# Block-recurrent attention with top-1 experts: batches' weights in half-MB parts, one per slot, and deeper buffers for the rounds

## The chip, the cores and the metric

The kernel runs on one core of a Trainium2 chip. The metric is the device time of one execution in microseconds, as the median of several runs. Engines are called PE (matrix), DVE (vector), ACT (scalar), POOL (GpSimd) and SP (which here only issues transfers).

## The reference

There are eight batches with eight heads each. Every head has 512 tokens `x` and 32 states, 64 wide. Tokens attend to the states and states attend to the tokens. The results are joined to 544 rows of 512 per batch (512 token rows, 32 state rows), 4352 rows in all. Every row then goes to one of eight experts, by the largest gate logit, and through that expert's two layers.

```python
scores = x @ state.T / 8;   xread = softmax(scores) @ state      # 512 token rows
scores2 = state @ x.T / 8;  sread = softmax(scores2) @ x         # 32 state rows
x = concat([xread, sread]) as (4352, 512)
e = argmax(x @ w_gate);     gate = softmax(x @ w_gate)[e]
out = gate * (relu(x @ w1[e]) @ w2[e])                           # w1: 8 x 512 x 1024, w2: 8 x 1024 x 512
```

All numbers are 32-bit floats. One expert's `w1` has 2 MB, and so has its `w2`.

## The kernel before, in words

**Token rows by batch.** The kernel takes the expert that most token rows of a batch chose (`eb`) for the whole batch; a branch at the end would mend batches in which rows chose otherwise, and with this data it isn't entered. It never forms `xread`: `states_w1` multiplies the states with `w1` (tile `G`, 32 matmuls named pG), `up` multiplies the attention weights `aT` with `G` (ph, 32 matmuls of 512 columns) and applies relu into `hT`, and `down` multiplies `hT` with `w2` (py, four column blocks `c` of 16 matmuls in two halves), after which ACT scales a block into `y` and issues its store. One batch is `down(b)`, with `states_w1(b + 1)` in it, and then `up(b + 1)`. `w1` has one buffer, `w2` two, `y` three.

**Slots.** `others()` is one generator that holds all the rest of the work in program order. `down` advances it eight times (after the first half and after the end of each block) and `up` four times, so a batch has 12 slots. Slots 0 to 27 are the attention of batches 1 to 7 (`first`, `front`, `back`). Slots 28 and 29 sort the state rows by expert and scatter them to DRAM (`sort_states`), and then `change_pools` gives the attention's memory to the rounds.

**State rows by rounds.** Three rounds of 128 sorted state rows follow, four groups of 32 rows with an expert each. A round reads 8 tiles of `w1` (tag s1) and 8 of `w2` (tag s2). Each tile is 1 MB and comes by four transfers of 256 KB (`s<-in_moe_w_dram`), one per group. `rounds` first fetches as many tiles as there are buffers (`S1B, S2B = 3, 3`) with the gathered rows `xg` between them, lets five slots go by, and then has `round_x` (ptx), four `round_up` (pgh, 16 matmuls) with a slot between two of them, relu, `round_h` (pth), and four times two `round_down` (pgy, 8 matmuls each). After each `round_up` two s1 tiles are fetched, after each `round_down` one s2 tile.

**Order.** Engines keep the program's order (`InOrder`). All reads are issued on SP, the `y` stores on ACT. Before, `load_w1` and `load_w2` issue 2 MB at once, in `between(c)` after block 2 (block 3 of batch 0) and after `down`. `between(c)` runs after the slot at the end of a block:

```python
store(c, py)
if insert:
    next(insert, None)      # the slot's work
if between:
    between(c)              # states @ w1 of the next batch, load of w1 after it
```

Four PSUM banks, `bank(...)`, serve py, ph, pG and the attention's small results in turn; `states_w1` takes all four, and each is free again when ACT has copied it to `G`.

**Start.** `begin()` chooses batch 0's expert from the states alone, loads its `w1` in two column halves, then `x` and states of batch 1, then `w2`, and writes blank rows to DRAM (four transfers), all on SP.

In the profile every instruction stands under line 48, the helper that records it, so groups are told by their tiles.

Of the kernel before, what the change touches and what calls it, by code (L numbers as in the profile page):

```python
# [9 lines left out]
FP32 = mybir.dt.float32  # L10
# [10 lines left out]
def kernel(  # L21
# [36 lines left out]
    DM = H * D  # L58
# [12 lines left out]
    NG = 16  # L71
    NR = NG // 4
    NRS = 3
    S1B, S2B = 3, 3
    FAR = 1 << 20

    PSUM = bass.MemoryType.PSUM
# [2 lines left out]
    wpool = ctx.enter_context(tc.tile_pool(name="wpool", bufs=1))  # L80

    ss_dram = dram.tile([NG * 32, XW], I32)


    ffn = tc.alloc_tile_pool(name="ffn", bufs=1)
# [22 lines left out]
    load_x(0, sp)  # L108
    wg = const.tile([128, NDC, E], FP32)
    act.dma_start(out=wg[:], in_=moe_w_gate.rearrange("(c p) e -> p c e", p=128))  # L110
    warm = const.tile([128, 1], FP32)
    dve.memset(warm[:], 0.0)
    act.activation(warm[:], warm[:], AF.Exp)
# [40 lines left out]

    aT = const.tile([128, B, 4, 2, 128], FP32)

    stT = const.tile([128, B, H, 2, NS], FP32)
    NX = B * NC  # L160
    lgs = const.tile([128, NST, E], FP32)
    oh = const.tile([128, NX + NST, E], BF16)
# [35 lines left out]

    def turn_states(b, copy):

        to = stT[:, b].rearrange("p h u n -> p (h u n)")
        dve.transpose(to[0:64], st2[b][:].rearrange("p h d -> p (h d)"))
        copy(to[64:128], to[0:64])

    def states_gates(b):

        pg = [bank("pg") for _ in range(2)]
        for q in range(4):
            for g in range(2):
                pe.matmul(pg[g][ts(q, 32), 0:E], lhsT=stT[ts(g, 64), b, 2 * q + g, 0, :],  # L210
                          rhs=wg[ts(g, 64), q, :], start=True, stop=True, skip_group_check=True)
        for g in range(2):
            act.copy(gst[:, b, g, 0:E], pg[g][:, 0:E])

    def scores(b, xt):

        pc = ps_c.tile([128, 4, 512], FP32, tag="c", name="pc")
        for g in range(2):
            for u in range(2):
                for q in range(4):  # L220
                    for i in range(4):
                        pe.matmul(pc[ts(q, 32), i, ts(g, 128)], lhsT=stT[ts(i, 32), b, 2 * q + g, u ^ (i % 2), :],
                                  rhs=xt[ts(i, 32), 2 * q + g, :, u, :],
                                  start=(u == 0), stop=(u == 1), skip_group_check=True)
        return pc
# [95 lines left out]
            load_states(b + 2, sp, sp)  # L321

    def turn_read(b, i=ALL):
        dve.transpose(aT[:, b, i].rearrange("p i g s -> p (i g s)"),
                      soft[b][0][:, i].rearrange("p i b n -> p (i b n)"))

    def logits_x(b):
        pl = bank("pl")[:, 0:128]
        for g in range(2):
            for i in range(4):  # L330
                pe.matmul(pl[ts(i, 32)], lhsT=gst[:, b, g, :], rhs=aT[:, b, i, g, :],
                          start=(g == 0), stop=(g == 1), skip_group_check=True)
# [79 lines left out]
    def begin():  # L412

        nonlocal G, hT
        turn_states(0, act.copy)
        states_gates(0)
        pr = bank("prg")[:, 0:E]
        for g in range(2):
            pe.matmul(pr, lhsT=ones_f[:], rhs=gst[:, 0, g, 0:E], start=(g == 0), stop=(g == 1), skip_group_check=True)
        xt, sx = new_xt(), new_sx()  # L420
        turn_x(0, xt, slice(0, 4))
        most(0, pr)
        e = expert_of(eb, 0)
        load_w1(0, e, 2)
        load_x(1, sp)
        load_states(1, sp, sp)
        load_w2(0, e)
        for r in range(NR):
            sp.dma_start(out=ss_dram[ts(r, 128)], in_=blank[:])
        turn_x(0, xt, slice(4, 8))  # L430
        pc = scores(0, xt)
        one, two = slice(0, 2), slice(2, 4)
        soft[0] = (sx,)
        turn_scores(pc, sx, 0)
        turn_scores(pc, sx, 1)
        less_max(sx, one, dve)
        exponential(sx, one)
        turn_scores(pc, sx, 2)
        turn_scores(pc, sx, 3)
        over_sum(sx, one, dve)  # L440
        turn_read(0, one)
        G = states_w1(w1s[0], stT[:, 0])
        less_max(sx, two, dve)
        exponential(sx, two)
        nm = write_max(pc)
        over_sum(sx, two, dve)
        turn_read(0, two)
        hT = new_hT()
        up(G, aT[:, 0], hT, one)
        soft[0] += write_weights(pc, nm)  # L450
        xt, sx = new_xt(), new_sx()
        turn_x(1, xt, slice(0, 4))
        turn_x(1, xt, slice(4, 8))
        turn_states(1, act.copy)
        exps, gates = logits_x(0)

        def beside():
            states_gates(1)
            pc = scores(1, xt)
            for i in range(4):  # L460
                turn_scores(pc, sx, i)
# [12 lines left out]
            yield  # L474
        up(G, aT[:, 0], hT, two, beside(), 4)

    def expert_of(table, i, engines=(SP,)):
        _, (e,) = nc.values_load_multi_w_load_instructions(
# [3 lines left out]

    w1s, w2s = {}, {}

    def load_w1(b, e, parts=1):
        w1s[b] = wpool.tile([128, NDC, F], FP32, tag="w1", name="w1t")
        for k in range(parts):
            f = ts(k, F // parts)
            sp.dma_start(out=w1s[b][:, :, f], in_=moe_w1[ds(e, 1)].rearrange("o (c p) f -> p (o c) f", p=128)[:, :, f])

    def load_w2(b, e):
        w2s[b] = wpool.tile([128, NFC, DM], FP32, tag="w2", bufs=2, name="w2t")
        sp.dma_start(out=w2s[b][:], in_=moe_w2[ds(e, 1)].rearrange("o (c p) f -> p (o c) f", p=128))

    def run(*gens):

# [17 lines left out]
    def states_w1(w1t, st):  # L514

        G = ffn.tile([128, 2, F], FP32, tag="G", name="G")
        for k in range(2):
            pg = [bank("pG") for _ in range(2)]
            for q in range(4):
                for g in range(2):  # L520
                    pe.matmul(pg[g][ts(q, 32), :], lhsT=st[ts(g, 64), 2 * q + g, 0, :],
                              rhs=w1t[ts(g, 64), q, ts(k, 512)], start=True, stop=True, skip_group_check=True)
            for g in range(2):
                act.copy(G[:, g, ts(k, 512)], pg[g][:])
        return G
# [17 lines left out]
    def down(hT, w2t, store, insert=None, between=None):  # L543
        for c in range(NC):
# [5 lines left out]
                    next(insert, None)  # L550
            store(c, py)
            if insert:
                next(insert, None)
            if between:
                between(c)

    def store_batch(b):
        rows = out[ds(b * SO, S)].rearrange("(p c) f -> p c f", c=NC)
# [172 lines left out]
    def rounds(r0, r1):  # L731
# [3 lines left out]
        fetch(S1B, 0)  # L735
        round_in(r0)
        fetch(0, S2B)
        for _ in range(5):
            yield
        for r in range(r0, r1):  # L740
            round_x(r)
# [14 lines left out]
            for f in range(0, NFC, 2):  # L756
                for i in range(2):
                    round_down(r, f + i)
                    fetch(0, 1)
                yield  # L760
                if r + 1 < r1:
                    yield
            round_out(r)


# [2 lines left out]
    def first():  # L768
# [6 lines left out]
        write_rows(1)  # L775
        choose(1)
        e1 = expert_of(eb, 1)
        load_w1(1, e1)
        load_w2(1, e1)
        gates()  # L780
        yield
        for b in range(2):
            turned[b] = turn_rows(b)

    turned = {}

    def others():

# [9 lines left out]
    def batch(b):  # L798
# [3 lines left out]
        def between(c):  # L802
            nonlocal G
            if c == (1 if b else 2) and b + 1 < B:
                G = states_w1(w1s[b + 1], stT[:, b + 1])
            if c == (2 if b else 3) and b + 2 < B:
                load_w1(b + 2, expert_of(eb, b + 2))

        down(hT, w2s[b], store_batch(b), work, between)
        if b + 2 < B:  # L810
            load_w2(b + 2, expert_of(eb, b + 2))
        if b + 1 < B:
            hT = up(G, aT[:, b + 1], new_hT(), insert=work)

    work = others()
    for b in range(B):
        batch(b)
# [8 lines left out]
    with tc.If(number(rest_i, B * S + NG) > 0):  # L826
# [3 lines left out]
        with tc.If(number(left_i, B * S) > 0):  # L830
# [18 lines left out]
            with tc.For_i(0, n_pairs, 1):  # L849
# [15 lines left out]
                bb = expert_of(pb, 0, [DVE])  # L865
                load_w1("x", e)
                load_w2("x", e)
                a_x = late["sst"].tile([128, 1, 4, 2, 128], FP32, tag="s1", bufs=S1B, name="a_x")
                dve.tensor_copy(out=a_x[:], in_=aT[:, ds(bb, 1)])
                st_x = late["sst"].tile([128, 1, H, 2, NS], FP32, tag="s2", bufs=S2B, name="st_x")  # L870
                dve.tensor_copy(out=st_x[:], in_=stT[:, ds(bb, 1)])
# [16 lines left out]
                def store(c, py):  # L888
# [5 lines left out]
                down(up(states_w1(w1s["x"], st_x[:, 0]), a_x[:, 0], new_hT()), w2s["x"], store)  # L894
            fix.release()

    for pool in (late["ps_t"], late["ps_g"], late["sst"], ps_p, ffn):
# [31 lines left out]
```

## Time and profile before

| | |
|---|---|
| median of 3 runs | 503.45 us (501.69 to 507.53) |
| profiled execution | 502.99 us, its span 501.2 us |
| PE busy | 465.6 us, 93% of the span |
| DVE, ACT, POOL busy | 119.2, 123.9, 33.9 us |
| moved by DMA | 105.77 MB, 211 GB/s over the span |

PE is the engine that is nearly always busy; the rest is idle time before its instructions, which the timeline gives in brackets with what ended it. A group of matmuls that waits inside for its operands shows as a longer group, not as idle time. The 1.8 us between span and time lie outside the profile.

### The profile page before, as it was taken

How to read it: one execution, taken by the hardware profiler on the slowest of the kernel's cores; microseconds unless marked ns; L12 is line 12 of the kernel's file. 1: busy time of each engine (PE TensorE's matmuls, PEld its weight loads, DVE VectorE, ACT ScalarE, POOL GpSimd, SP SyncE). 2: the span in 40 equal slices, each digit the busy share in tenths (PEclk: the TensorE clock that was granted, in tenths of full speed). 3: DMA queues.
4: the chain of work that ended last, by engine and by line, in shares of the span. 5: the costliest groups of instructions: out<-in, count | busy, mean ns of one | idle time of the engine just before them, and what ended most of it. 6: DMA issues, size and time to landing. Idle time of an engine off the chain costs nothing.

```text
span 501.2 us, 8606 instructions
## 1 busy us (share of the span) xinstructions
PE 465.6 (93%) x3445; PEld 208.1 (42%) x3445; DVE 119.2 (24%) x302; ACT 123.9 (25%) x257; POOL 33.9 (7%) x39
## 2 busy tenths in 40 slices
PE   2699899999899999984999999998999999999995
PEld 2386555455355544431334333432433343343342
DVE  4747565656547623100000000000000000000000
ACT  1244143541415422220032112022120221311101
POOL 1000032230202210100000000000000000000000
PEclk9999999999999999998799999999999999999999
DMA  4942397943535001899769968599558998319211
GB/s 106 355 152 73 95 320 226 337 112 122 190 122 193 4 27 43 279 366 384 272 212 329 391 221 284 180 382 364 196 190 293 397 307 264 118 34 343 72 42 45
DMA packets 63821, 105.77 MB, mean 211 GB/s; under 512 B 11935, under 2 KB 21151, under 8 KB 63776
## 3 DMA queue, kind: packets, MB, share of 16 engines
q1 hardware_dynamic: 57696, 95.64, 56.0%
q10 hardware_dynamic: 5680, 8.47, 4.7%
q0 software_dynamic: 400, 1.05, 0.6%
q8 instruction: 29, 0.48, 0.4%
q14 instruction: 16, 0.13, 0.1%
HBM read 94.13 MB, written 10.75 MB: 209 GB/s over the span
## 4 chain that ended last, share of the span: by engine, by line
PE 73%; DMA 15%; DVE 4%; SPq 3%; issue 2%; ACT 1%; POOL 0%; ACTq 0%; DVEq 0%; POOLq 0%
PE py L48 39%; PE ph L48 15%; DMA s<-in_moe_w_dram 9%; PE pgy L48 5%; DMA w1t<-in_moe_w_dram 4%; PE pgh L48 4%; PE pG L48 3%; PE pc L48 3%; SPq L48 3%; PE pw L48 2%; PE pt L48 2%; DVE xt L48 1%; DMA xg<-ss_dram 1%; DMA st<-in_state_dram 1%; PE pl L48 1%
## 5 line engine op out<-in xcount | busy, mean ns | idle before, releaser
L48 PE MATMUL py<-w2t,hT 128*128 128x512 f32 x512 | 230.8, 601 | 2.5 <-ACT G L48 2.0
L48 PEld LDWEIGHTS py<-w2t,hT 128*128 128x128 f32 x512 | 94.4, 191 | 126.6 <-issue 112.2
L48 PE MATMUL ph<-aT,G 128*128 128x512 f32 (+1 forms) x288 | 117.6, 559 | 0.0
L48 PEld LDWEIGHTS ph<-aT,G 128*128 128x128 f32 x288 | 54.1, 194 | 55.6 <-issue 52.8
L48 ACT ACTIVATE y<-py,gw 128x512 f32<-128x512 f32 x32 | 22.0, 687 | 211.1 <-PE py L48 197.2
L48 ACT ACTIVATE hT<-ph 128x512 f32<-128x512 f32 (+1 forms) x72 | 39.2, 550 | 93.7 <-PE ph L48 93.6
L48 DVE COPY shT<-pth 128x512 f32<-128x512 f32 x3 | 2.1, 692 | 160.6 <-PE pth L48 160.6
L48 PE MATMUL pgh<-s,sxT 128*32 128x512 f32 x192 | 30.0, 619 | 9.4 <-DMA s<-in_moe_w_dram 9.4
L48 PE MATMUL pgy<-s,shT 128*32 128x512 f32 x192 | 27.5, 599 | 0.6 <-DMA s<-in_moe_w_dram 0.6
L48 DVE TENSOR_SCALAR ys<-pgy,xg 128x512 f32<-128x512 f32 x3 | 2.3, 752 | 91.9 <-PE pgy L48 91.9
L48 PE MATMUL pG<-w1t,stT 64*32 64x512 f32 x256 | 18.4, 653 | 4.2 <-DMA w1t<-in_moe_w_dram 4.2
L48 POOL DMA_INDIRECT out_dram<-ys,xg x3 | 2.9, 971 | 263.2 <-DVE ys L48 102.9
L48 DVE STREAM_TRANSPOSE xt<-x_nat 128x1024 f32<-128x1024 f32 x16 | 19.5, 1227 | 1.1 <-DMA x_nat<-in_x_dram 1.1
L48 PE MATMUL pc<-xt,stT 32*32 32x128 f32 x1024 | 17.0, 295 | 2.8 <-issue 1.4
L48 ACT COPY G<-pG 128x512 f32<-128x512 f32 x32 | 16.5, 599 | 11.4 <-PE pG L48 11.4
L48 PEld LDWEIGHTS pgh<-s,sxT 128*32 128x32 f32 x192 | 6.2, 110 | 30.6 <-DMA s<-in_moe_w_dram 17.3
L48 DVE STREAM_TRANSPOSE sx<-pc 128x256 f32<-128x256 f32 x32 | 11.7, 419 | 26.4 <-PE pc L48 26.4
L48 PEld LDWEIGHTS pc<-xt,stT 32*32 32x32 f32 x1024 | 13.5, 107 | 4.1 <-DVE xt L48 1.8
L48 PEld LDWEIGHTS pgy<-s,shT 128*32 128x32 f32 x192 | 6.1, 109 | 20.2 <-issue 14.7
L48 POOL TENSOR_TENSOR sx<-sx,mx 128x1024 f32<-128x1024 f32 x6 | 11.5, 1910 | 34.8 <-DVE mx L48 34.8
L48 DVE STREAM_TRANSPOSE aT<-sx 128x1024 f32<-128x1024 f32 (+1 forms) x9 | 10.1, 1127 | 12.4 <-POOL sx L48 12.3
L48 POOL TENSOR_TENSOR sx<-sx,sm 128x1024 f32<-128x1024 f32 x6 | 11.5, 1912 | 23.0 <-DVE sm L48 19.4
(118 smaller groups left out, 214.0 us busy)
## 6 DMA issues: line engine op xcount, KB each, us to landing
s<-in_moe_w_dram SPq DMA_DIRECT2D x192, 256.0 KB, 5.2
w2t<-in_moe_w_dram SPq DMA_DIRECT2D x8, 2048.0 KB, 12.9
w1t<-in_moe_w_dram SPq DMA_DIRECT2D x7, 2048.0 KB, 10.3
x_nat<-in_x_dram SPq DMA_DIRECT2D x16, 512.0 KB, 5.6
out_dram<-y ACTq DMA_DIRECT2D x32, 256.0 KB, 3.4
w1t<-in_moe_w_dram SPq DMA_DIRECT2D x2, 1024.0 KB, 6.8
ss_dram<-blank SPq DMA_DIRECT2D x4, 257.0 KB, 8.5
xg<-ss_dram SPq DMA_DIRECT2D x3, 257.0 KB, 4.6
```

Of the source, the lines that this page charges most:

```text
L48: ins = getattr(self.engine, name)(*args, **kw)
```

## The change

Batches' weights: `w1_parts` and `w2_parts` give four transfers of half a MB each (`w1` by rows of 128, so a row of 4 KB stays whole; `w2` by two rows of 2 KB). They stand in a list, `lazy`, and each slot issues one of them after its other work. `w1(b + 2)` is put there after block 1 (block 3 of batch 0), `w2(b + 2)` after `down`. Batch 0's `w1` keeps its two halves; `w1` of batch 1 is issued at once. `states_w1` runs ahead of the slot's work at the end of a block. The rounds have 5 and 4 buffers, wait 7 slots, and the last round has the slots of the others. The space comes from the attention: `aT` of batches 0 to 2 and all transposed states `stT` lie in its pool; a packed copy of the states, `stG`, is made by two POOL copies per batch for `states_w1`; and since the branch at the end needs `aT` of any batch, each is also written to DRAM (`at_dram`, 512 KB per batch, on SP). In `begin`, states of batch 1 are loaded at the very start, `w2` comes right behind `w1`, and `x` of batch 1 is issued on ACT behind the first exponential.

```diff
-    S1B, S2B = 3, 3
+    S1B, S2B = 5, 4
+    at_dram = dram.tile([B, 128, 1024], FP32)
@@ start
     act.dma_start(out=wg[:], in_=moe_w_gate.rearrange("(c p) e -> p c e", p=128))
+    load_states(1, sp, sp)
@@ turn_states
+        stT[b] = att.tile([128, H, 2, NS], FP32, tag="stT", bufs=2, name="stT")
         dve.transpose(to[0:64], st2[b][:].rearrange("p h d -> p (h d)"))
         copy(to[64:128], to[0:64])
+        for g in range(2):
+            gp.tensor_copy(out=stG[ts(g, 64), b], in_=stT[b][:].rearrange("p (q g) u n -> p g u q n", g=2)[ts(g, 64), g, 0])
@@ turn_read
+        if b not in aT:
+            aT[b] = att.tile([128, 4, 2, 128], FP32, tag="aT", bufs=NE, name="aTe")[:]
...
+        if i.stop == 4:
+            sp.dma_start(out=at_dram[b], in_=aT[b].rearrange("p i g s -> p (i g s)"))
@@ begin
-        load_w1(0, e, 2)
-        load_x(1, sp)
-        load_states(1, sp, sp)
-        load_w2(0, e)
+        at_once(w1_parts(0, e, 2))
+        at_once(w2_parts(0, e))
...
         exponential(sx, one)
+        load_x(1, act)
...
-        G = states_w1(w1s[0], stT[:, 0])
+        G = states_w1(w1s[0], stG[:, 0])
@@
+    def w1_parts(b, e, cols=1):
+        t = w1s[b] = wpool.tile([128, NDC, F], FP32, tag="w1", name="w1t")
+        rows = moe_w1[ds(e, 1)].rearrange("o (c p) f -> p (o c) f", p=128)
+        f = F // cols
+        return [lambda k=k: sp.dma_start(out=t[:, :, ts(k, f)], in_=rows[:, :, ts(k, f)]) for k in range(cols)] if cols > 1 else \
+            [lambda k=k: sp.dma_start(out=t[:, k], in_=rows[:, k]) for k in range(NDC)]
+    def w2_parts(b, e):
+        t = w2s[b] = wpool.tile([128, NFC, DM], FP32, tag="w2", bufs=2, name="w2t")
+        rows = moe_w2[ds(e, 1)].rearrange("o (c p) f -> p (o c) f", p=128)
+        return [lambda k=k: sp.dma_start(out=t[:, ts(k, 2)], in_=rows[:, ts(k, 2)]) for k in range(NFC // 2)]
@@ down
             if insert:
+                step = between(c)
+                next(step)
                 next(insert, None)
-            if between:
-                between(c)
+                next(step)
@@ rounds
-        for _ in range(5):
+        for _ in range(7):
             yield
...
-                if r + 1 < r1:
-                    yield
+                yield
@@ first
-        load_w1(1, e1)
-        load_w2(1, e1)
+        at_once(w1_parts(1, e1))
+        lazy.extend(w2_parts(1, e1))
@@ batch
             if c == (1 if b else 2) and b + 1 < B:
-                G = states_w1(w1s[b + 1], stT[:, b + 1])
-            if c == (2 if b else 3) and b + 2 < B:
-                load_w1(b + 2, expert_of(eb, b + 2))
+                G = states_w1(w1s[b + 1], stG[:, b + 1])
+            yield
+            if c == (1 if b else 3) and b + 2 < B:
+                lazy.extend(w1_parts(b + 2, expert_of(eb, b + 2)))
+            yield
-        down(hT, w2s[b], store_batch(b), work, between)
+        down(hT, w2s[b], store_batch(b), slots, between)
         if b + 2 < B:
-            load_w2(b + 2, expert_of(eb, b + 2))
+            lazy.extend(w2_parts(b + 2, expert_of(eb, b + 2)))
...
+    def with_weights():
+        while True:
+            next(work, None)
+            if lazy:
+                lazy.pop(0)()
+            yield
```

## Rows read from the trace of the kernel before

**Rows 1.** The page: busy time of the engines, and the chain that ended last.

```profile
PE 465.6 (93%) x3445; PEld 208.1 (42%) x3445; DVE 119.2 (24%) x302; ACT 123.9 (25%) x257; POOL 33.9 (7%) x39
PE 73%; DMA 15%; DVE 4%; SPq 3%; issue 2%; ACT 1%; POOL 0%; ACTq 0%; DVEq 0%; POOLq 0%
```

**Rows 2.** Timeline of PE, rounds: start, us, operation, count, [idle before <- releaser].

```profile
216.94 0.63 PE L48 MATMUL ptx<-ident,xg 128*128 128x128 f32 x4 [1.89 <-DMA s<-in_moe_w_dram]
...
220.93 1.92 PE L48 MATMUL pgh<-s,sxT 128*32 128x512 f32 x16
222.78 7.13 PE L48 MATMUL py<-w2t,hT 128*128 128x512 f32 x16
...
238.26 3.90 PE L48 MATMUL pgh<-s,sxT 128*32 128x512 f32 x8 [7.34 <-DMA s<-in_moe_w_dram]
242.08 7.77 PE L48 MATMUL py<-w2t,hT 128*128 128x512 f32 x16
...
284.34 3.08 PE L48 MATMUL pgy<-s,shT 128*32 128x512 f32 x8 [0.55 <-DMA s<-in_moe_w_dram]
...
349.37 3.45 PE L48 MATMUL pgh<-s,sxT 128*32 128x512 f32 x8 [2.05 <-DMA s<-in_moe_w_dram]
...
453.57 3.02 PE L48 MATMUL pgy<-s,shT 128*32 128x512 f32 x16
```

**Rows 3.** Windows: stretch, us, busy by engine, granted clock, DMA share, GB/s.

```profile
200.84:225.47 24.63, 22.74 (x69) 9.48 (x68) 1.75 (x12) 6.05 (x10) 2.14 (x2) 1.00 0.94 327
...
197.70:204.70 7.00, 7.00 (x21) 3.18 (x18) 4.36 (x28) 0.90 (x2) 2.14 (x2) 1.00 0.42 132
...
222.80:238.30 15.50, 8.16 (x29) 3.15 (x26) 0.00 (x0) 0.69 (x1) 0.00 (x0) 0.83 1.04 381
...
212.70:222.20 9.50, 7.61 (x30) 3.01 (x32) 0.00 (x0) 2.97 (x5) 0.00 (x0) 1.00 1.01 366
```

**Rows 4.** Timeline of SP's issues before the longest wait, and ACT's store among them.

```profile
220.34 0.39 SPq L48 DMA_DIRECT2D w1t<-in_moe_w_dram  x1
221.30 0.38 SPq L48 DMA_DIRECT2D w2t<-in_moe_w_dram  x1
222.82 3.73 SPq L48 DMA_DIRECT2D xg<-ss_dram  x1
226.82 4.25 SPq L48 DMA_DIRECT2D s<-in_moe_w_dram  x5
...
237.42 6.74 SPq L48 DMA_DIRECT2D s<-in_moe_w_dram  x11
...
230.67 0.36 ACTq L48 DMA_DIRECT2D out_dram<-y  x1
```

**Rows 5.** Timelines of PE and ACT around states @ w1 of batches 1 and 2.

```profile
72.95 1.10 PE L48 MATMUL pw<-x_nat,a2T 128*32 128x64 f32 x64
...
74.42 1.95 PE L48 MATMUL pG<-w1t,stT 64*32 64x512 f32 x32
...
126.90 2.36 PE L48 MATMUL pG<-w1t,stT 64*32 64x512 f32 x32
131.25 3.70 PE L48 MATMUL py<-w2t,hT 128*128 128x512 f32 x8 [1.99 <-ACT G L48]
...
130.62 2.04 ACT L48 COPY G<-pG 128x512 f32<-128x512 f32 x4
```

**Rows 6.** Timelines of PE and ACT, start: first products with w1.

```profile
19.70 1.96 PE L48 MATMUL pG<-w1t,stT 64*32 64x512 f32 x16 [2.35 <-DMA w1t<-in_moe_w_dram]
21.59 8.81 PE L48 MATMUL ph<-aT,G 128*128 128x256 f32 x32
...
17.44 1.07 ACT L48 COPY G<-pG 128x512 f32<-128x512 f32 x2 [0.94 <-PE pG L48]
```

**Rows 7.** Timeline of POOL: one of eight copies of states.

```profile
54.67 0.60 POOL L48 COPY stT<-stT 64x512 f32<-64x512 f32 x1 [51.75 <-DVE stT L48]
```

**Rows 8.** All transfers of the rounds' weights: time from issue to landing.

```profile
DMA to landing us min/median/max: 2.4/5.2/12.6
```

More of the change, by code (lines that the diff above doesn't have):

```diff
@@ L153 @@
         dve.tensor_scalar(tok_s[:, g:g + 1], tmp_p[:], float(4 * g * SO + S), None, ALU.add)
-    aT = const.tile([128, B, 4, 2, 128], FP32)
-    stT = const.tile([128, B, H, 2, NS], FP32)
+    NE = 3
+    aTl = const.tile([128, B - NE, 4, 2, 128], FP32)
+    aT = {b: aTl[:, b - NE] for b in range(NE, B)}
+    stT = {}
+    stG = const.tile([128, B, 4, NS], FP32)
     NX = B * NC
@@ L199, in turn_states @@
     def turn_states(b, copy):
[L201 removed]
+        stT[b] = att.tile([128, H, 2, NS], FP32, tag="stT", bufs=2, name="stT")
+        to = stT[b][:].rearrange("p h u n -> p (h u n)")
         dve.transpose(to[0:64], st2[b][:].rearrange("p h d -> p (h d)"))
         copy(to[64:128], to[0:64])
+        for g in range(2):
+            gp.tensor_copy(out=stG[ts(g, 64), b], in_=stT[b][:].rearrange("p (q g) u n -> p g u q n", g=2)[ts(g, 64), g, 0])
     def states_gates(b):
@@ L209, in states_gates @@
             for g in range(2):
-                pe.matmul(pg[g][ts(q, 32), 0:E], lhsT=stT[ts(g, 64), b, 2 * q + g, 0, :],
+                pe.matmul(pg[g][ts(q, 32), 0:E], lhsT=stT[b][ts(g, 64), 2 * q + g, 0, :],
                           rhs=wg[ts(g, 64), q, :], start=True, stop=True, skip_group_check=True)
@@ L221, in scores @@
                     for i in range(4):
-                        pe.matmul(pc[ts(q, 32), i, ts(g, 128)], lhsT=stT[ts(i, 32), b, 2 * q + g, u ^ (i % 2), :],
+                        pe.matmul(pc[ts(q, 32), i, ts(g, 128)], lhsT=stT[b][ts(i, 32), 2 * q + g, u ^ (i % 2), :],
                                   rhs=xt[ts(i, 32), 2 * q + g, :, u, :],
@@ L323, in turn_read @@
     def turn_read(b, i=ALL):
-        dve.transpose(aT[:, b, i].rearrange("p i g s -> p (i g s)"),
+        if b not in aT:
+            aT[b] = att.tile([128, 4, 2, 128], FP32, tag="aT", bufs=NE, name="aTe")[:]
+        dve.transpose(aT[b][:, i].rearrange("p i g s -> p (i g s)"),
                       soft[b][0][:, i].rearrange("p i b n -> p (i b n)"))
+        if i.stop == 4:
+            sp.dma_start(out=at_dram[b], in_=aT[b].rearrange("p i g s -> p (i g s)"))
     def logits_x(b):
@@ L330, in logits_x @@
             for i in range(4):
-                pe.matmul(pl[ts(i, 32)], lhsT=gst[:, b, g, :], rhs=aT[:, b, i, g, :],
+                pe.matmul(pl[ts(i, 32)], lhsT=gst[:, b, g, :], rhs=aT[b][:, i, g, :],
                           start=(g == 0), stop=(g == 1), skip_group_check=True)
@@ L448, in begin @@
         hT = new_hT()
-        up(G, aT[:, 0], hT, one)
+        up(G, aT[0], hT, one)
         soft[0] += write_weights(pc, nm)
@@ L474, in beside @@
             yield
-        up(G, aT[:, 0], hT, two, beside(), 4)
+        up(G, aT[0], hT, two, beside(), 4)
     def expert_of(table, i, engines=(SP,)):
@@ L483, with at_once @@
     w1s, w2s = {}, {}
[L485 to L493, printed above, removed]
+    def w1_parts(b, e, cols=1):
[8 more added lines that the diff above has]
+        return [lambda k=k: sp.dma_start(out=t[:, ts(k, 2)], in_=rows[:, ts(k, 2)]) for k in range(NFC // 2)]
+    def at_once(parts):
+        for p in parts:
+            p()
     def run(*gens):
@@ L520, in states_w1 @@
                 for g in range(2):
-                    pe.matmul(pg[g][ts(q, 32), :], lhsT=st[ts(g, 64), 2 * q + g, 0, :],
+                    pe.matmul(pg[g][ts(q, 32), :], lhsT=st[ts(g, 64), q, :],
                               rhs=w1t[ts(g, 64), q, ts(k, 512)], start=True, stop=True, skip_group_check=True)
@@ L783, in first @@
             turned[b] = turn_rows(b)
-    turned = {}
+    turned, lazy = {}, []
     def others():
@@ L804, in between @@
             if c == (1 if b else 2) and b + 1 < B:
-                G = states_w1(w1s[b + 1], stT[:, b + 1])
-            if c == (2 if b else 3) and b + 2 < B:
-                load_w1(b + 2, expert_of(eb, b + 2))
-        down(hT, w2s[b], store_batch(b), work, between)
+                G = states_w1(w1s[b + 1], stG[:, b + 1])
[4 more added lines that the diff above has]
+        down(hT, w2s[b], store_batch(b), slots, between)
         if b + 2 < B:
-            load_w2(b + 2, expert_of(eb, b + 2))
+            lazy.extend(w2_parts(b + 2, expert_of(eb, b + 2)))
         if b + 1 < B:
-            hT = up(G, aT[:, b + 1], new_hT(), insert=work)
+            hT = up(G, aT[b + 1], new_hT(), insert=slots)
+    def with_weights():
[4 more added lines that the diff above has]
+            yield
+    slots = with_weights()
     work = others()
@@ L864 @@
                 e = expert_of(px, 0)
[L865 to L871, printed above, removed]
+                bb = expert_of(pb, 0, [SP, DVE])
+                at_once(w1_parts("x", e))
+                at_once(w2_parts("x", e))
+                a_x = late["sst"].tile([128, 4, 2, 128], FP32, tag="s1", bufs=S1B, name="a_x")
+                sp.dma_start(out=a_x[:].rearrange("p i g s -> p (i g s)"),
+                             in_=at_dram[ds(bb, 1)].rearrange("o p s -> p (o s)"))
+                st_x = late["sst"].tile([128, 1, 4, NS], FP32, tag="s2", bufs=S2B, name="st_x")
+                dve.tensor_copy(out=st_x[:], in_=stG[:, ds(bb, 1)])
                 g_x = fix.tile([128, NC, 1], FP32)
@@ L893, in store @@
                         in_=y[:], in_offset=None, bounds_check=NTOK - 1, oob_is_err=False)
-                down(up(states_w1(w1s["x"], st_x[:, 0]), a_x[:, 0], new_hT()), w2s["x"], store)
+                down(up(states_w1(w1s["x"], st_x[:, 0]), a_x[:], new_hT()), w2s["x"], store)
             fix.release()
```

## The prediction

> **What bounds the kernel now.** I read the page first: PE is busy for 465.6 us of the 501.2 us span, and the chain that ended last is PE for 73% and transfers for 15% [rows 1]. Beside PE and its weight loads no engine is busy for a third of the span. So the time is PE's work, plus what PE waits. The change removes no matmul; it can only take away waits or add some. So I read PE's timeline for groups with idle time before them, and for groups that are longer than others of their kind, and noted which wait ended each.
>
> Three places stand out. First, the rounds. A round_up without waits is a group of 16 in 1.92 us, so 8 take 0.96 us; a block of py takes 7.13 us [rows 2]. Against these:
> - the first round_x waits 1.89 us (for xg: the releaser named is a tile of weights, but the matmul reads xg);
> - the second round_up waits 7.34 us, its second half then takes 3.90 instead of 0.96, and the py block behind it 7.77 instead of 7.13: 7.34 + 2.94 + 0.64 = 10.92 us;
> - a round_down half waits 0.55 us and takes 3.08: 2.67 us;
> - a round_up half waits 2.05 us and takes 3.45: 4.54 us;
> - four groups have no idle time but are longer; the one shown takes 3.02 instead of 1.92, 1.10 us, and with the other three (1.31, 0.49 and 0.60) it is 3.50 us.
> The sum is 1.89 + 10.92 + 2.67 + 4.54 + 3.50 = 23.5 us. The longest wait has its cause in SP's timeline: `w1` and `w2` of batch 4, 4 MB, are issued at 220.34 and 221.30, ahead of the s1 tile that PE waits for, which is issued from 226.82 [rows 4]. In that stretch the transfers run at 381 GB/s [rows 3], so 4.2 MB are 11 us in front of the tile. And the granted clock's mean over that stretch is 0.83, after PE had begun to wait.
>
> Second, pG of batch 2, in batch 1's `down`: its group takes 2.36 instead of 1.95 us, and py waits 1.99 us behind it, because ACT copies `G` only from 130.62 on, behind the attention's exponentials of that slot [rows 5]. That is 2.40 us. Third, the start, where PE waits for the halves of batch 0's `w1` [rows 6]; the change doesn't shorten that.
>
> **The rounds, part by part.** *More buffers.* With three s1 buffers, after a round_up one tile of the next is there and the other has to be issued, moved and landed within two slots. With five, both are there and the fetch has until the round_up after that: two slots and a round_up more, about 9 us, or 3.4 MB at 381 GB/s. With four s2 buffers instead of three the same holds for a pair of round_down. *Parts.* 2 MB at 381 GB/s are 5.5 us ahead of a tile; half a MB is 1.4 us. *Is there bandwidth?* From 200.84 on the rounds read 48 tiles (50 MB), batches 4 to 7 some 17 MB, and stores take 5 MB: 72 MB, or 190 us at 381 GB/s of the 270 us that are left. So the waits come from order and depth, not from bytes, and I take all 23.5 us as removed, except at the start of the rounds.
>
> *The start of the rounds.* Now 5 + 4 tiles (9.4 MB) are issued in one slot on SP, and three of the four parts of `w1` of batch 4 come behind them in SP's order. What must land by the last of these: 9.4 MB of tiles, 0.3 of xg, 0.5 of scatter, 0.5 of stores, 1.6 of parts: 12.3 MB. Before, the first 24.63 us moved 327 GB/s, 8.05 MB [rows 3]; the other 4.3 MB at 381 GB/s take 11.2 us, which is 236.7, and about 237.7 with the landing. PE comes to this `states_w1` when? Round_x would have run at 216.94 - 1.89 = 215.05 [rows 2]; from there half a 7.13 remains of `up`, then two blocks of `down`, ptx and a round_up: 3.6 + 14.2 + 0.5 + 1.92, so 235.3. The wait is 237.7 - 235.3 = 2.4; I take +2.5 us. Its bounds are 0 (at 381 GB/s throughout it lands at 234) and some 10 us, the first rival. `w2` of batch 4 (5.5 us more) lands near 243 and the next s1 pair near 249, and PE needs the second tile of it at 250.3: just in time.
>
> *Seven slots, and four more slots in the last round.* Two more slots are 7 us at least, which covers the 1.89 us for xg. The rounds end in slot 88 of 92 instead of 83, with three halves of py (10.7 us) behind the last round_down; its DVE scaling and store wait for no slot, so the tail doesn't grow. PE's work is the same in another order: 0.
>
> **The rest.** *States @ w1 first.* Its four copies come on ACT ahead of the slot's exponentials, and the slot's other matmuls give them time. This removes the 2.40 us: -2.4, with 0.4 more if batch 3's pG, as long in the trace, shortens too. Price: batch 1's own `w1` is wanted earlier by pw and pl, 74.42 - 72.95 = 1.47 us, and before it had no idle time [rows 5]; between 0 and 1.47, I take 0.5.
>
> *Batch 1's x on ACT.* Here the change adds a wait. The rows show how many transfers are in flight: behind w2t at 221.30 come xg, five of s and one store on ACT, and then SP issues nothing until 237.42 [rows 4], though the next tile has no part in w2t. So a transfer waits for the eighth before it, on whichever engine. In `begin` the order after w1 is four parts of w2, four blanks, the two halves of x: x's halves wait for w2's first and second part, and ACT stands still with the copies of `G` and the next exponential queued behind. w1's second half is there at 19.70 [rows 6]; 1.4 us per part gives 21.1 and 22.5, and with the issue 23.0. The copies that ran at 17.44 (1.07 us) would then end at 24.1, and ph start there instead of at 21.59: +2.5 us. If x's issue comes ahead of the blanks in that order, the wait is for something long landed: 0. I take 1.5, nearer to the written order.
>
> *Transposed states, packed copies, aT to DRAM.* Two POOL copies per batch of a quarter of the columns of one that takes 0.60 us [rows 7]; nothing waits for POOL just behind them: 0 to 0.6 us each if they were on the path, taken at 0, as `states_w1` comes half a batch later. Eight writes of 0.5 MB are 1.4 us of transfer each, in the attention's stretch. SP waits there for DVE's transpose, with the slot's part and the next state-row writes behind it; these wait for the same stretch of work anyway. At most 1.4 us on a tie, twice; I take 0.3 in all. The states of batch 1 at the start: behind batch 0's x, 0.
>
> **Sum**, against the profiled execution of 502.99 us (the median of the runs, 503.45, is 0.1% above it): 502.99 - 23.5 + 2.5 - 2.4 + 0.5 + 1.5 + 0.3 = 481.9. I predict 482 us.
>
> **A rule against it.** Where the rounds' 256 KB transfers run alone, from 212.70 to 222.20, they move 366 GB/s; the stretch with the two 2 MB ones in it moves 381 [rows 3]. The Trainium skill ("DMA: Bandwidth & Descriptors", "Rules for kernel authors") asks for 128 partitions and at least 1 MiB per transfer for the highest bandwidth; these parts have half of that. By that rule it is the fourth rival; the two rows leave 4% for it, since transfers of a quarter of that size queue behind each other without a gap.
>
> **Rivals.**
> 1. *The start of the rounds still starves.* The 12.3 MB move at 280 GB/s instead of 341: 44 us, 245.8 with the landing, a wait of 10.5 us, and the clock falls as it did before (0.83, 0.64 us on the next block and more on the half round), with the next s1 pair 2 us late. 482 + 8 + 3 = 493. For it: 132 GB/s from 197.70 to 204.70, against it: 327 over the whole start [rows 3]. 14%.
> 2. *The waits move and don't vanish*, because transfers are what bounds the rounds. Then deeper buffers only shift them: 499 to 503 us. For it: a DMA share of 1.04 where PE waited [rows 3]; against it the 72 MB in 270 us above. 7%.
> 3. *Slower: the burst blocks batch 4's w1.* One place, as in 1, but the burst keeps the poor rate of its first microseconds, since scatter, store and tiles meet there. It decides the sign below 216 GB/s: 12.3 MB then take 57 us and PE waits over 21 us more. At 200 GB/s it is 61.5 us, a wait of 28 us and half clock behind it: 508. 4%.
> 4. *Half-MB parts don't overlap.* The shortest landing of a 256 KB transfer is 2.4 us [rows 8], so a part alone takes some 3.1 us instead of 1.4. That binds where parts lie behind the burst: three of w1, 5 us, and four of w2, 7 us, of which 3 are slack: 482 + 9 = 491. 5%.
>
> **How the numbers follow.** The forecast has 70%, between 476 (no new wait at all) and 488 (the start at +2.5, the rounds' start at +5, ties in the attention). A change under 1%, 5 us, could not be told from none in this kernel. Faster by over 1%: the forecast, rivals 1 and 4, 0.89; within 1%: rival 2, 0.07; slower: rival 3, 0.04. The range from 475 to 494 holds the forecast and most of rivals 1 and 4.
>
> **What would show it.** In the changed profile, PE should have no idle time over 1 us before pgh or pgy, and their groups of 16 should take 1.92; the clock should stay at 1.00 through 225 to 250. There should be one wait of 1 to 5 us before pG of batch 4, ended by w1t. Batch 1's py should not wait for `G`. On ACT, x's issue in the start should stand for some 5 us ahead of the copies of `G`, with ph from 22 to 24. The prediction is wrong if a wait over 5 us is left in the rounds, or if PE's busy time itself grows.

## The result

The changed kernel takes 483.67 us (median of 4 runs, 482.35 to 485.41), the kernel before beside it 504.38 us (4 runs, 501.69 to 507.53): a ratio of 0.9589, interval 0.9523 to 0.9655. In a second comparison, with other runs of both, it was 480.73 against 501.73 us, 0.9557, 0.949 to 0.9625. The forecast was 482, with 475 to 494 as its range. The profiled execution took 485.41 us, its span is 483.6 us, and the granted clock is 1.00 over all of it.

### The profile page after: what moved, and what is told of

Same layout as the page of the kernel before. It is cut to its first block, busy times and chain, and to the rows that moved or that the text cites. A ratio compares the mean times of both kernels' runs of the same rounds, so it can differ in the third digit from the quotient of the medians.

```text
span 483.6 us, 8760 instructions
## 1 busy us (share of the span) xinstructions
PE 457.8 (95%) x3445; PEld 206.1 (43%) x3445; DVE 119.4 (25%) x302; ACT 123.5 (26%) x257; POOL 38.6 (8%) x55
## 4 chain that ended last, share of the span: by engine, by line
PE 80%; DMA 11%; DVE 4%; issue 2%; ACT 1%; SPq 1%; POOL 1%; ACTq 0%; POOLq 0%; DVEq 0%
PE py L48 40%; PE ph L48 20%; DMA s<-in_moe_w_dram 5%; PE pgy L48 5%; PE pgh L48 4%; DMA w1t<-in_moe_w_dram 3%; PE pc L48 3%; PE pG L48 2%; PE pt L48 2%; PE pw L48 2%; DMA wg<-in_moe_w_gate_dram 1%; DVE xt L48 1%; DMA out_dram<-y 1%; SPq L48 1%; PE pl L48 1%
## 5 line engine op out<-in xcount | busy, mean ns | idle before, releaser
L48 PE MATMUL ph<-aTl,G 128*128 128x512 f32 x160 | 71.5, 597 | 0.0
L48 PEld LDWEIGHTS ph<-aTl,G 128*128 128x128 f32 x160 | 29.6, 190 | 40.2 <-issue 39.7
L48 PE MATMUL ph<-aTe,G 128*128 128x256 f32 (+1 forms) x128 | 46.3, 514 | 0.0
L48 PEld LDWEIGHTS ph<-aTe,G 128*128 128x128 f32 x128 | 24.9, 202 | 16.6 <-issue 13.7
L48 PE MATMUL pG<-w1t,stG 64*32 64x512 f32 x256 | 21.6, 654 | 4.6 <-DMA w1t<-in_moe_w_dram 4.4
L48 PE MATMUL pgh<-s,sxT 128*32 128x512 f32 x192 | 23.1, 598 | 0.0
L48 PE MATMUL pgy<-s,shT 128*32 128x512 f32 x192 | 23.1, 598 | 0.0
L48 PEld LDWEIGHTS pG<-w1t,stG 64*32 64x32 f32 x256 | 4.6, 109 | 18.9 <-issue 12.9
```

Source lines behind the costliest of these rows:

```text
L48: ins = getattr(self.engine, name)(*args, **kw)
```

## The profile after

The page of the changed kernel: busy time by engine; the chain that ended last; three groups (busy, mean ns | idle before them).

```profile
PE 457.8 (95%) x3445; PEld 206.1 (43%) x3445; DVE 119.4 (25%) x302; ACT 123.5 (26%) x257; POOL 38.6 (8%) x55
...
PE 80%; DMA 11%; DVE 4%; issue 2%; ACT 1%; SPq 1%; POOL 1%; ACTq 0%; POOLq 0%; DVEq 0%
...
L48 PE MATMUL pG<-w1t,stG 64*32 64x512 f32 x256 | 21.6, 654 | 4.6 <-DMA w1t<-in_moe_w_dram 4.4
...
L48 PE MATMUL pgh<-s,sxT 128*32 128x512 f32 x192 | 23.1, 598 | 0.0
L48 PE MATMUL pgy<-s,shT 128*32 128x512 f32 x192 | 23.1, 598 | 0.0
```

PE has the same 3445 matmuls, but is busy for 7.8 us less, and its idle time fell from 35.6 to 25.8 us [rows 1]. Both come from waits: a group that waits inside for its operands counts as busy, and so does one that runs slower behind a wait (from 234 to 242 us of the kernel before, the granted clock was 0.50, the lower level of 1.2 GHz). The rounds' two kinds of group have no idle time left, and 12 groups of 16 at 1.92 us make the 23.1 us of each. What is new is in pG: it is busy for 21.6 us where it was 18.4. Of the 4.6 us idle before it 0.46 are new, at batch 4; the rest is the start's, which the kernel before had too (4.2).

PE's timeline at the start of the rounds, answering [rows 2]: start, us, operation, count, [idle before].

```profile
226.08 0.63 PE L48 MATMUL ptx<-ident,xg 128*128 128x128 f32 x4 [1.65 <-DMA s<-in_moe_w_dram]
...
230.07 1.92 PE L48 MATMUL pgh<-s,sxT 128*32 128x512 f32 x16
231.93 7.13 PE L48 MATMUL py<-w2t,hT 128*128 128x512 f32 x16
238.99 1.37 PE L48 MATMUL pG<-w1t,stG 64*32 64x512 f32 x8
240.59 1.05 PE L48 MATMUL pG<-w1t,stG 64*32 64x512 f32 x4 [0.22 <-DMA w1t<-in_moe_w_dram]
241.88 1.91 PE L48 MATMUL pG<-w1t,stG 64*32 64x512 f32 x20 [0.24 <-DMA w1t<-in_moe_w_dram]
243.71 1.92 PE L48 MATMUL pgh<-s,sxT 128*32 128x512 f32 x16
```

The second round_up, which waited 7.34 us before, now takes 1.92 with nothing ahead of it. Two waits are left: 1.65 us before the first round_x, and `states_w1` of batch 4, which comes in pieces as the parts of its `w1` land. It lasts from 238.99 to 243.79, 4.80 instead of 1.95 us, so 2.85.

SP's issues in that stretch, answering [rows 4], and the window of [rows 3] again.

```profile
203.29 15.40 SPq L48 DMA_DIRECT2D s<-in_moe_w_dram  x20
219.01 0.33 SPq L48 DMA_DIRECT2D xg<-ss_dram  x1
219.60 12.69 SPq L48 DMA_DIRECT2D s<-in_moe_w_dram  x16
232.63 1.86 SPq L48 DMA_DIRECT2D w1t<-in_moe_w_dram  x3
236.46 2.26 SPq L48 DMA_DIRECT2D w2t<-in_moe_w_dram  x4
```

```profile
222.80:238.30 15.50, 13.85 (x47) 5.58 (x46) 0.00 (x0) 1.27 (x2) 0.00 (x0) 1.00 1.03 379
```

The transfers are as busy as before (379 GB/s), yet PE is busy for 13.85 of the 15.50 us instead of 8.16, at a granted clock of 1.00 (2.4 GHz) instead of a mean of 0.83. What SP's rows show is the price: xg is issued only when 20 transfers of s1 are, and the three parts of `w1` only when 36 of both kinds are.

PE's timeline around states @ w1 of batches 1 and 2, answering [rows 5], and after it SP's issues of batch 1's weights (first the changed kernel, then the one before).

```profile
74.30 3.63 PE L48 MATMUL pG<-w1t,stG 64*32 64x512 f32 x32
...
130.16 0.70 PE L48 MATMUL py<-w2t,hT 128*128 128x512 f32 x1 [1.35 <-issue]
130.78 1.95 PE L48 MATMUL pG<-w1t,stG 64*32 64x512 f32 x32
...
133.60 3.70 PE L48 MATMUL py<-w2t,hT 128*128 128x512 f32 x8
```

```profile
66.49 2.65 SPq L48 DMA_DIRECT2D w1t<-in_moe_w_dram  x4
```

```profile
64.74 0.40 SPq L48 DMA_DIRECT2D w1t<-in_moe_w_dram  x1
```

Batch 2's pG is 1.95 us and py waits no longer for `G`. Batch 1's pG takes 3.63, 1.68 us more: PE comes to it before pw and pl, while its `w1` now takes four issues, which last 2.65 us instead of 0.40. The whole `w1` landed 9.0 us after its issue, at 73.8, 0.7 us ahead of pG; the last of the four parts lands 7.2 us after its own, at 76.0, when pG has been running for 1.7 us.

The start, PE and ACT, answering [rows 6].

```profile
8.04 0.33 PE L48 MATMUL pg<-wg,stT 64*32 64x8 f32 x16 [8.04 <-DMA wg<-in_moe_w_gate_dram]
...
20.43 1.96 PE L48 MATMUL pG<-w1t,stG 64*32 64x512 f32 x16 [1.85 <-DMA w1t<-in_moe_w_dram]
22.32 9.26 PE L48 MATMUL ph<-aTe,G 128*128 128x256 f32 x32
```

```profile
16.69 0.95 ACTq L48 DMA_DIRECT2D x_nat<-in_x_dram  x2
18.64 1.07 ACT L48 COPY G<-pG 128x512 f32<-128x512 f32 x2 [1.33 <-PE pG L48]
```

The two issues of x take 0.95 us on ACT, and the copy behind them waited for PE's pG, not for them. Still ph starts 0.73 us later than before: the first instruction of PE waited until 8.04, for the gate's weights, where it began at 7.23 before, with DVE's `xt` as the last that it waited for.

## Experiments

The theory that I set out with: the waits in the rounds come from order and depth, and the deeper buffers are needed for the gain (depth theory). Its rival: the order of the issues is enough, and the buffers only bring the two new waits with them (order theory). Kernels in one group ran side by side, with the kernel before among them (500.75, 501.73 and 501.04 us in the three groups); across groups, ratios are compared. No kernel leaves out any of the computation.

### First group: undo one part of the change

**Three buffers again.**

```diff
-    S1B, S2B = 5, 4
+    S1B, S2B = 3, 3
```

> The changed kernel with three s1 and three s2 buffers again; all else stays. Theory depth (the prediction's: with three buffers one tile of the next step must still be fetched within two slots, and that is what starved the rounds): waits before pgh and pgy come back, of the order of half of the 23.5 us, so about 493 us, and groups of 16 longer than 1.92 us in all three rounds. Theory place (the waits came from 4 MB of batch weights in front of an urgent tile, and from a first fetch with too little time; with parts and seven slots three buffers are enough): within 3 us of the changed kernel, 481 to 487 us, and perhaps less wait at batch 4's w1, since 3 MB less stand in front of it.

Measured: 478.22 us, 0.9536 (0.9506 to 0.9566), by the ratios not slower than the whole change. PE and SP at the start of the rounds:

```profile
221.84 0.60 PE L48 MATMUL ptx<-ident,xg 128*128 128x128 f32 x4
...
234.72 1.95 PE L48 MATMUL pG<-w1t,stG 64*32 64x512 f32 x32
236.60 2.77 PE L48 MATMUL pgh<-s,sxT 128*32 128x512 f32 x16
```

```profile
211.05 0.33 SPq L48 DMA_DIRECT2D xg<-ss_dram  x1
...
219.56 1.68 SPq L48 DMA_DIRECT2D w1t<-in_moe_w_dram  x3
```

The first fetch has 24 transfers instead of 36, so xg is issued 8.0 us earlier and the parts of batch 4's `w1` 13.1 us earlier; 2.4 us of either is that this execution came to the rounds earlier (its first fetch starts at 200.86). Both new waits are gone, and for want of depth only one round_up is longer, by 0.85 us. As a need for depth, the theory falls here.

**Whole loads.** Everything of the change, but each `w1` and `w2` by one transfer of 2 MB, in the slot of its first part.

```diff
-            [lambda k=k: sp.dma_start(out=t[:, k], in_=rows[:, k]) for k in range(NDC)]
+            [lambda: sp.dma_start(out=t[:], in_=rows)]
...
-        return [lambda k=k: sp.dma_start(out=t[:, ts(k, 2)], in_=rows[:, ts(k, 2)]) for k in range(NFC // 2)]
+        return [lambda: sp.dma_start(out=t[:], in_=rows)]
```

> The changed kernel with each load of 2 MB in one piece, issued in the slot in which its first part went; buffers, slots and order stay. Theory size (2 MB in front of a tile are 5.5 us): waits of 2 to 4 us before some pgh or pgy, about 488 us. Theory place: with five and four buffers 5.5 us are covered, so nothing new there, and the whole w1 of batch 4 now goes ahead of the rounds' first fetch, so its wait of 2.85 us goes: 481 us. Rule of 1 MiB per transfer: faster by its own account too, but with shorter landings for the same bytes everywhere.

Measured: 481.38 us, 0.9599 (0.9567 to 0.9631). No group of the rounds waits, batch 4's pG isn't longer (its `w1` is issued whole at 192.63, ahead of the first fetch), and the round_x wait is 1.04 us. Beside five and four buffers the parts give nothing that these runs can tell.

**Five slots of lead.**

```diff
-        for _ in range(7):
+        for _ in range(5):
```

> The changed kernel with five slots ahead of the first round_x instead of seven (the rounds end two slots sooner). xg lay 1.65 us late with seven slots, and two slots are 7 us: a wait of 8 to 9 us before ptx, less the wait at batch 4's w1, which then lies behind it: 488 to 491 us. If xg's lateness is only a matter of its place behind the tiles and not of time, no change.

Measured: 489.15 us, 0.9752 (0.9708 to 0.9795), some 8 to 10 us over the whole change by the ratios. The timeline of PE, and two windows, in the wait and behind it (the granted clock is the third number from the end):

```profile
222.19 1.09 PE L48 MATMUL ptx<-ident,xg 128*128 128x128 f32 x4 [7.34 <-DMA s<-in_moe_w_dram]
```

```profile
218.00:222.00 4.00, 0.00 (x0) 0.00 (x0) 0.00 (x0) 0.00 (x0) 0.00 (x0) 0.77 0.99 354
222.00:224.00 2.00, 1.81 (x6) 1.32 (x7) 0.00 (x0) 0.59 (x1) 0.00 (x0) 0.50 1.05 399
```

round_x comes two slots earlier, but xg still stands behind 20 transfers: 7.34 us. In that wait the clock falls to 0.50, and the 8 matmuls behind round_x take 5.53 us instead of 3.60. I had costed the seven slots at the 1.89 us of xg; beside the deep first fetch they carry about five times that.

**The slot's work first**, as before, in place of states @ w1.

```diff
                 step = between(c)
+                next(insert, None)
                 next(step)
-                next(insert, None)
                 next(step)
```

> The changed kernel with states @ w1 behind the slot's work again, and nothing else changed. Theory: the wait before py of batch 1 (2.4 us with the longer pG) comes back, and the wait of 1.68 us within pG of batch 1 goes, since w1 of batch 1 lands only when that slot begins; at batch 4 pG comes 1.9 us later, which takes as much off its wait. Net within 1.5 us of the changed kernel, 482 to 485 us.

Measured: 479.54 us, 0.9572 (0.9536 to 0.9608), the same as the whole change. PE's timeline at the pG of batches 2 and 4:

```profile
126.65 2.36 PE L48 MATMUL pG<-w1t,stG 64*32 64x512 f32 x32
131.00 3.70 PE L48 MATMUL py<-w2t,hT 128*128 128x512 f32 x8 [1.99 <-ACT G L48]
...
237.99 2.16 PE L48 MATMUL pG<-w1t,stG 64*32 64x512 f32 x32
```

The 2.40 us are back to the hundredth, so they were this order's; batch 1's pG is 1.95 again, so its 1.68 us were too. And batch 4's pG, which comes behind the second round_up here, takes 2.16 us instead of 4.80. At these three places the change's order thus lost 1.68 + 2.64 - 2.40, some 1.9 us, which is less than these runs can tell.

### Second group: one part alone

**Only the lead**, on the kernel before.

```diff
-        for _ in range(5):
+        for _ in range(7):
```

> The kernel before, with seven slots ahead of the first round_x instead of five; nothing else. Theory place and lead: the 1.89 us before ptx go, and of the 10.92 us at the second round_up the 7 us that the two slots give; the waits of rounds 0 to 2 behind it (2.67, 4.54, 3.50) and the 2.40 us before py of batch 1 stay: 0.98 of before. If lead alone were enough: 0.96.

Measured: 496.18 us, 0.9857 (0.9783 to 0.9931): by the medians 5.5 us of the gain for a single number. The wait for xg is gone (1.89 us), and at the second round_up the idle time and the longer half come to 6.60 us instead of 10.28; the two make 5.6:

```profile
239.67 4.30 PE L48 MATMUL pgh<-s,sxT 128*32 128x512 f32 x8 [3.26 <-DMA s<-in_moe_w_dram]
```

**Three buffers and whole loads**, with the rest of the change.

> The changed kernel with three and three buffers and whole 2 MB loads: what is left in the rounds is the lead, the slot in which a batch's loads are issued, and the last round's slots. Theory place: little more wait than with parts, within 2 us of the run with three buffers and parts (0.954 of before). Theory size: with so few buffers 5.5 us in front of a tile show, waits of 2 to 4 us in each round: 0.97.

Measured: 484.65 us, 0.9657 (0.9586 to 0.9729). With parts it was 0.9536, so beside three buffers the parts are worth some 6 us, by the ratios. In its profile one round_up shows 3.5 us of them (1.38 of waiting, and 3.08 instead of 0.96 for 8 matmuls):

```profile
331.34 3.08 PE L48 MATMUL pgh<-s,sxT 128*32 128x512 f32 x8 [1.38 <-DMA s<-in_moe_w_dram]
```

By PE's positions the two profiles differ by 4.5 us at the end, 1.4 of it ahead of the rounds; the rest of the 6 us no profile shows.

So with neither parts nor depth the kernel has 17 of the 21 us that the whole change has in this group. Against the kernel with only the lead, waits and longer groups of the rounds come to 4.0 us instead of 17.6, and 15.0 of the 17.6 lay in the first two rounds, ahead of the slots that were added to the last. What differs there in SP's issues is the slot of the loads. With only the lead, `w1` and `w2` of batch 4 go together behind the rounds' first fetch; here `w1` goes 30 us ahead of `w2`, and ahead of that fetch:

```profile
221.06 0.39 SPq L48 DMA_DIRECT2D w1t<-in_moe_w_dram  x1
222.38 0.38 SPq L48 DMA_DIRECT2D w2t<-in_moe_w_dram  x1
```

```profile
191.27 0.39 SPq L48 DMA_DIRECT2D w1t<-in_moe_w_dram  x1
...
221.10 0.40 SPq L48 DMA_DIRECT2D w2t<-in_moe_w_dram  x1
```

No run moved the loads and nothing else, so that this slot is the reason is argued from these rows, not shown.

**The order alone**: the kernel before with parts, one per slot; states @ w1 ahead of the slot's work, but not for batch 1; seven slots; the last round with the slots of the others. Three buffers, memory, start, and the states' and `aT`'s places as before.

```diff
...
-            if c == (1 if b else 2) and b + 1 < B:
+            if b and c == 1 and b + 1 < B:
                 G = states_w1(w1s[b + 1], stT[:, b + 1])
...
+            yield
+            if b == 0 and c == 2:
+                G = states_w1(w1s[1], stT[:, 1])
+            if c == (1 if b else 3) and b + 2 < B:
+                lazy.extend(w1_parts(b + 2, expert_of(eb, b + 2)))
+            yield
...
```

> The kernel before with the changes of order alone: parts one per slot, states @ w1 ahead of the slot's work (for batch 1 behind it), seven slots, the last round's slots. Buffers, the attention's memory, the loads at the start stay; no copies on POOL, no aT in DRAM. Theory place: all of the gain and up to 2 us more than the changed kernel with three buffers: 0.950 of before. If depth, the copies or the start gave some of it: between 0.96 and 0.98.

Measured: 478.21 us, 0.9527 (0.9459 to 0.9594), the lowest ratio of all. Two round_ups are longer, by 0.71 and 1.43 us:

```profile
234.22 2.63 PE L48 MATMUL pgh<-s,sxT 128*32 128x512 f32 x16
...
243.85 3.35 PE L48 MATMUL pgh<-s,sxT 128*32 128x512 f32 x16
```

**The changed kernel once more**, beside it.

> The changed kernel beside these on one chip: 0.959 of before, as at first. Should it come out at 0.954, three buffers give nothing against five and four.

Measured: 480.73 us, 0.9557 (0.949 to 0.9625). The two waits at the rounds' start are there again, the second as a pG of batch 4 that is 3.76 us longer:

```profile
224.48 0.63 PE L48 MATMUL ptx<-ident,xg 128*128 128x128 f32 x4 [1.20 <-DMA s<-in_moe_w_dram]
```

The order alone is 2.5 us faster by the medians, but the intervals overlap. It isn't seen to be slower, and more is not settled.

### Third group: what is left, and a repeat

**The order alone with five slots** (the same edit as above).

> The kernel before with the changes of order, but five slots ahead of the first round_x: parts, the slot of the loads and states @ w1 first without the lead. Alone, the lead gave 5.5 us on the kernel before. If it gives the same beside the parts: 484 us, with the wait at the second round_up back at 4 to 7 us. If the parts had already taken what the lead gives: 479 us. If lead and parts need each other: 488 us or more.

Measured: 484.49 us, 0.9657 (0.9631 to 0.9683). The repeat below has 479.38, so here the lead is worth 5.1 us, about what it was alone. Behind 1.28 us before round_x, the second round_up waits again:

```profile
232.26 4.28 PE L48 MATMUL pgh<-s,sxT 128*32 128x512 f32 x8 [3.30 <-DMA s<-in_moe_w_dram]
```

**The first fetch of s2 spread over the last slots of the lead**, one tile per slot, in the order alone and in the changed kernel. In the first the question is whether place can remove its two longer round_ups, in the second whether the burst is what holds back batch 4's `w1`.

```diff
-        fetch(0, S2B)
-        for _ in range(7):
+        for i in range(7):
             yield
+            if i >= 7 - S2B:
+                fetch(0, 1)
```

> The order-only kernel with the three s2 tiles of the first fetch issued one per slot, in the last three of the seven. What is left there is 0.71 us at the first and 1.43 us at the second round_up. If these come from the place of the s2 tiles in front: both go, 476 us. If they come from the bytes that must land by then, whatever their order: no change, 478 us.

Measured: 479.62 us, 0.9557 (0.9531 to 0.9583): no gain. The two groups are still longer, by 1.27 and 0.17 us:

```profile
236.29 3.19 PE L48 MATMUL pgh<-s,sxT 128*32 128x512 f32 x16
...
246.47 2.09 PE L48 MATMUL pgh<-s,sxT 128*32 128x512 f32 x16
```

> The changed kernel (five and four buffers) with the four s2 tiles of the first fetch issued one per slot, in the last four of the seven; parts of batch 4's w1 go ahead of them. Theory: its wait of 2.85 us goes, and that before ptx (1.2 to 1.7 us) stays, since xg stands behind the s1 tiles as before: 478 us. If the deep first fetch is not what holds w1 back: 481 us. If depth is of use anywhere in the rounds, this kernel is then faster than order alone.

Measured: 479.85 us, 0.9564 (0.9536 to 0.9592). SP's issues, and PE's timeline behind them:

```profile
218.02 0.33 SPq L48 DMA_DIRECT2D xg<-ss_dram  x1
218.64 1.76 SPq L48 DMA_DIRECT2D w1t<-in_moe_w_dram  x3
```

```profile
224.07 0.63 PE L48 MATMUL ptx<-ident,xg 128*128 128x128 f32 x4
...
236.98 1.95 PE L48 MATMUL pG<-w1t,stG 64*32 64x512 f32 x32
...
250.53 1.68 PE L48 MATMUL pgh<-s,sxT 128*32 128x512 f32 x4 [0.84 <-DMA s<-in_moe_w_dram]
```

The parts of `w1` are issued 14.0 us earlier, and batch 4's pG doesn't wait: the 16 transfers of s2 were the cause of that wait. xg is still behind 20 of s1, but issued 1.0 us earlier than in the first profile; it lands 5.8 us later, 0.2 us before PE comes to it. In their place one round_up waits inside, 0.84 us and some stretching. That the time hardly moves shows how little is left to gain here.

**The order alone once more.**

> The order-only kernel again, beside these on one chip: 0.953 of before, as at first; it is what the others of this call are read against.

Measured: 479.38 us, 0.9545 (0.9518 to 0.9572), with the same two round_ups 1.36 and 0.94 us longer, and one of the second round by 1.58 us.

## Why the prediction was right, and which terms were off

In the profiled executions the time fell by 17.6 us, where the sum had 21.1. The waits of the rounds came out as forecast; the start, batch 2 and xg did not, by 1.3 to 1.7 us each. The measured column is worked out from PE's positions at the same matmul in both traces:

| | predicted | measured |
|---|---|---|
| start and batch 0, to the up of batch 1 | +1.5 + 0.5 | +3.4 |
| states @ w1 of batch 2 | -2.4 | -1.1 |
| to the rounds | +0.3 | +0.2 |
| rounds: waits of before, and all not named below | -23.5 | -23.8 |
| rounds: xg | 0 | +1.65 |
| rounds: w1 of batch 4 | +2.5 | +2.85 |
| from the last matmul to the end | 0 | -0.75 |
| sum | -21.1 | -17.6 |

**The waits in the rounds** went as forecast, and with them the low clock. Rivals 2 and 3 are out by the pgh and pgy rows and by the window; rival 1 by the 2.85 us where it had 10.5. Rival 4 had 3.1 us for a half-MB part that doesn't overlap with the next. In PE's timeline above, the last two parts of batch 4's `w1` release PE at 240.59 and 241.88, 1.3 us apart. And whole loads beside deep buffers are no faster (0.9599), beside three buffers slower (0.9657 against 0.9536). The Trainium skill ("DMA: Bandwidth & Descriptors", "Rules for kernel authors") asks for at least 1 MiB per transfer for the highest bandwidth. Here halves and quarters of a MB, queued behind each other, move 379 GB/s where 381 moved before.

**The step "More buffers" was not the cause.** The prediction took depth as a reason on the same footing as the parts. With three buffers and parts the kernel is as fast (0.9536), so the gain doesn't need depth. Nor is most of it the parts': with neither it is 0.9657. Beside whole loads depth takes away the waits that are left in the rounds (4.0 us in the profile with three buffers, none with five and four); whether it gains time there is not settled, as the intervals of 0.9599 and 0.9657 overlap. The lead of two slots is worth 5 to 6 us beside three buffers, where I had 1.89, since it also gives the second round_up time.

Depth has a price that I costed at +2.5 us for batch 4's `w1`. I overlooked that xg, between the s1 and the s2 tiles on the same queue, is pushed back by the two more s1 tiles: I took its 1.89 us as covered by the slots, and 1.65 came back, where three buffers leave none. That 2.85 us at pG is so close to 2.5 is luck: PE had already lost the 1.65 us ahead of it, so the last part came 4.5 us later than it was wanted. From the first issue of the fetch to that part it is 38.6 us, where I had 36.9; the rate was as worked out (342 GB/s, and I had 341).

**Batch 1's w1 wanted earlier**, +0.5 with 1.47 as upper bound, measured 1.68 us. The bound moved only the reader, and 0.65 us of it were slack. The change also moved the landing: measured from PE's work ahead of it, the last part comes 0.9 us later than the whole load did, and 1.47 - 0.65 + 0.9 makes 1.7. In the four other profiles with parts and this order pG is 0.8 to 2.6 us longer. In the two runs with whole loads it took 1.95 us, behind waits of 0.45 and 0.67 us, and in the one with the slot's work first 1.95 without a wait.

**x on ACT**, +1.5, was 0: it was the case of the two in which the issue waits for something long landed, and the sign that I had named, x's issue 5 us ahead of the copies of `G`, is absent. The start lost time elsewhere. PE's first wait (ended by the gate's weights, in the kernel before alone by DVE's `xt`) ended at 7.4 to 9.1 us in the eight profiles with batch 1's states loaded at the very start (mean 8.3), and at 6.9 to 8.1 in the six without (mean 7.3). The two sets overlap; a tendency of 1 us is what can be said, and that these loads cause it is not shown. The rest of the +3.4 us, beside the 1.68 of batch 1's pG, is 0.4 at ph of batch 0 and 0.5 in a longer gap of PE's own issue (1.90 instead of 1.42), beside small shifts. That these come to about the 1.5 us which I had for x is luck.

**States @ w1 first** removed its 2.40 us, as the run without it shows; it also brought PE to batch 4's `w1` a round_up earlier, which I hadn't priced. In the profile of after the issue gap just ahead is 1.35 us instead of 0.51, and pls waits 0.20 for `G`. In the other profiles with this order the gap is 0 to 1.1 us at the same place; what sets it I don't know.

**The terms at nothing.** POOL is busy for 4.7 us more. PE's pg now waits five times for 0.17 us on POOL's copy of the states, but from pxs to pc it is 0.79 us instead of 0.77 in four of these places; in the first it is 0.79 instead of 0.40. No wait of PE names the writes of `aT`, and the order alone, without them and the packed copies, is within the spread of the kernel that has them. I count them as the nothing that was forecast, up to some 2 us.

Open: what the slot of the loads gives by itself, the rest of the loss with three buffers and whole loads, the spread at the start, and whether the order alone is truly faster than the whole change.

## What to carry to other kernels

When a small load waits behind big ones on one queue, look first at when the big ones are issued, and ask of each remedy what it adds to the others before taking all of them. Here the kernel without parts and without depth had 17 of the 21 us; parts gave some 6 more beside three buffers, depth no more beside parts, and two more slots for the first fetch gave some 5 us and cost nothing. A deeper prefetch is itself a big load at the moment when it first fills: what stands behind it on its queue is late by as much, so put the urgent transfers ahead of it, or let it fill over several slots. And when a load is cut and its reader moved, bound the wait by both ends, the reader's new time and the last part's landing.

## What was not expected of the hardware

How long the rounds' fetch stays slow. The transfers of the changed kernel from 203 to 237 us, in 40 slices of 0.85 us:

```profile
DMA  0387869699999999999999989999999999999999
GB/s 0 70 260 210 113 224 254 244 369 377 396 357 362 410 383 390 400 381 337 347 337 306 342 292 350 359 407 405 400 390 386 388 386 386 364 376 386 383 393 381
```

The first eight slices, 6.8 us with the scatter of the state rows among them, have a mean of 172 GB/s; from the ninth on it is 292 to 410. The sum had this only in a mean over the whole start; rivals 1 and 3 named the slow beginning, but from a window that had begun 3 us ahead of the fetch. It falls on whatever is first in the queue, here the tiles ahead of xg. And of the clock: behind the 7.34 us wait of the run with five slots it was 0.50 (222 to 224 us), and behind the 3.26 us of the kernel with only the lead 0.57 in the mean (240 to 244), while through the 1.65 and 2.85 us of the changed kernel it stayed at 1.00 (225 to 250).
